# Copies of a k-v product moved ahead of a turned q, and six stores split in two

One NeuronCore of a Trainium2 chip runs the kernel. The metric is the device time of one execution in microseconds. The span in a profile is the time from the first to the last recorded instruction, some 1.8 us less. Times with three decimals are read from the trace's records, where the views round to two.

In the text and the profile lines, PE is the matmul engine, ScalarE (ACT) and VectorE (DVE) are the engines that copy and compute, GpSimd (POOL) is a fourth, and SP is the engine that issues most of the transfers (DMA). PSUM is the memory in which the PE leaves its results. A semaphore is a counter on which an instruction can wait; a wait is "held" while its counter is not there yet and "met" once it is. A transfer "lands" when its semaphore has its last update.

## The reference

Linear attention with cosine weights, then a SwiGLU block, over 4608 tokens:

```python
# q, k, v: (8, 8, 576, 64) float32; w_gate, w_val: (512, 1536); w_out: (1536, 512)
r = np.maximum(x, 0.0); phi = concat([r * cos_w, r * sin_w], axis=-1)    # for q and for k
kv = einsum('bhsf,bhsd->bhfd', k_p, v);  z = sum(k_p, axis=2)
attn = einsum('bhsf,bhfd->bhsd', q_p, kv) / (einsum('bhsf,bhf->bhs', q_p, z)[..., None] + 1e-06)
g = x @ w_gate                     # x: attn as (4608, 512)
out = (g / (1 + exp(-g)) * (x @ w_val)) @ w_out
```

## The kernel before

The program is laid out by hand: each engine executes its instructions in the order in which the code emits them. Two places matter.

The first is the end of the first group of tokens, where the second batch (b=1) gets ready. `kv_mm` makes its k-v products on the PE, `qturn_pe` turns its q on the PE and copies the turned q out of PSUM, `kv_out` copies the products out, and `a_half` multiplies the two:

```python
def qturn_pe(b, j, lo, hi, eng):
    ps = take(1) ...
    for c in range(lo, hi):
        nc.tensor.transpose(out=ps[:, c - lo], in_=st["qp"][:, b, c, j], identity=ident)   # L274
    copy_op(eng, qt_of(b)[...], ps[...])                                                   # L333
...
def kv_out(b, engs=("act", "dve"), js=slice(0, J)):
    for e, eng in enumerate(engs):
        for i in range(2):
            (nc.scalar.copy if eng == "act" else nc.vector.tensor_copy)(out=kvd[...], in_=ps[...])  # L297
...
at("b11", lambda: kv_mm(1), q_(1, 0, 0), q_(1, 1, 0, "dve"), lambda: kv_out(1))
at((0, 0), lambda: kv_free(1), a_(4, 0), a_(4, 1))
```

The second is the output. There are 36 tiles of 128 tokens. Each is copied from PSUM into one of four buffers `ob` and stored in two halves by SP. The last tile is made in two column pieces, each stored by SP and ScalarE together:

```python
obp = ctx.enter_context(tc.tile_pool(name="obp", bufs=4))
...
def ffn_out(t, f0=0, f1=None):
    ...
    (nc.scalar.copy if t % 2 == 0 else nc.vector.tensor_copy)(out=ob, in_=ps)                # L556
    for e in range(2):
        idx = 2 * t + e
        nc.sync.dma_start(out=out_v[idx // NC, idx % NC], in_=ob[e * SH:(e + 1) * SH])       # L559

def ffn_out_last(t):
    for lo, hi in ((0, 320), (320, d_model)):
        ...
        nc.scalar.copy(out=ob[:, 0:hi - lo], in_=ps)                                         # L571
        for e in range(2):
            idx = 2 * t + e
            (nc.sync if e else nc.scalar).dma_start(...)                                     # L574
```

The framework gives each transfer from SP and ScalarE one of eight semaphores, in turn. At the very end SP waits for all of them, first to eighth, one wait instruction each.

## Time and profile before

| | before |
|---|---|
| median of the runs beside the changed kernel | 324.99 us (324.85 to 325.15, 4 runs) |
| span of the profiled run | 323.204 us |
| PE busy | 98% |
| L549 goes on after the eight L444 of the first tile of batch two | 42.954 us |
| end of the last matmul | 319.219 us |
| last store lands | 321.850 us |
| from there to the end of the span | 1.354 us |

The PE is busy for 98% of the span, and it bounds the kernel but for a few places. So a gain must show in one of three numbers: the time at which L549 goes on after 41 us, the time between the last matmul and the last landing, or the time from that landing to the end. The prediction shows the lines of the profile from which these are read.

### The profile page before, as it was taken

The numbers are of one execution on the slowest core, as the hardware profiler recorded it, in microseconds if no ns is written. First come the engines' busy times: TensorE is split into PE (matmuls) and PEld (weight loads), VectorE is DVE, ScalarE is ACT, GpSimd is POOL, SyncE is SP. The second block draws the span as 40 slices with busy tenths as digits, with TensorE's granted clock in tenths as the row PEclk, the third lists the DMA queues.
The fourth block names the chain that finished last, engine by engine and source line by source line (L and its number), as shares of the span: only waits on it lengthen the run. The fifth ranks groups of instructions, "written<-read, shape, count | busy, mean of one in ns | idle before, by whom it ended". The sixth has DMA issues, their size and how long they took to land.

```text
span 323.2 us, 6031 instructions
## 1 busy us (share of the span) xinstructions
PE 316.1 (98%) x2384; PEld 159.0 (49%) x2384; DVE 180.9 (56%) x363; ACT 130.7 (40%) x239; POOL 35.3 (11%) x60
## 2 busy tenths in 40 slices
PE   7899999999999999999999999999999999999995
PEld 3596555454445444544454445444544444444443
DVE  7873766787448747564756555755573236323320
ACT  7553546662436345333533354335432132213311
POOL 6755002010101000110011000200000000000000
PEclk9999999999999999999999999999999999999999
DMA  7999997987995988599679968895912401240014
GB/s 267 215 200 197 206 194 136 213 113 108 178 200 79 184 152 134 79 175 177 116 97 160 164 123 118 134 184 109 134 36 48 103 14 35 50 103 11 0 32 97
DMA packets 74379, 41.01 MB, mean 127 GB/s; under 512 B 49904, under 2 KB 69104, under 8 KB 74352
## 3 DMA queue, kind: packets, MB, share of 16 engines
q1 hardware_dynamic: 52000, 22.95, 38.9%
q0 software_dynamic: 22192, 17.57, 36.6%
q8 instruction: 18, 0.29, 0.4%
q10 hardware_dynamic: 160, 0.13, 0.1%
q14 instruction: 9, 0.07, 0.1%
HBM read 37.75 MB, written 9.44 MB: 146 GB/s over the span
## 4 chain that ended last, share of the span: by engine, by line
PE 95%; ACT 2%; DVE 2%; issue 0%; ACTq 0%
PE banks L513 58%; PE banks L549 28%; PE banks L285 3%; PE banks L399 2%; PE banks L444 1%; PE banks L381 1%; DVE v L239 1%; PE banks L152 1%; PE banks L568 1%; PE banks L325 0%; PE banks L485 0%; ACT L184 0%; ACT phit L333 0%; PE banks L274 0%; ACT ob L571 0%; DVE qwT L369 0%
## 5 line engine op out<-in xcount | busy, mean ns | idle before, releaser
L524 DVE TENSOR_TENSOR ht<-sg,banks 128x512 bf16<-128x512 bf16 (+2 forms) x116 | 74.7, 650 | 68.7 <-PE banks L513 60.3
L513 PE MATMUL banks<-xT,wv_sb 128*128 128x512 bf16 (+2 forms) x464 | 111.3, 364 | 0.0
L513 PE MATMUL banks<-xT,wg_sb 128*128 128x512 bf16 (+2 forms) x464 | 111.3, 364 | 0.0
L519 ACT ACTIVATE sg<-banks 128x512 bf16<-128x512 f32 (+2 forms) x116 | 65.8, 568 | 111.6 <-PE banks L513 107.7
L549 PE MATMUL banks<-wo_sb,ht 128*128 128x512 bf16 x420 | 93.8, 379 | 0.0
L513 PEld LDWEIGHTS <-wv_sb 128*128 128x128 bf16 x464 | 44.8, 98 | 48.7
L513 PEld LDWEIGHTS <-wg_sb 128*128 128x128 bf16 x464 | 43.1, 98 | 42.8
L549 PEld LDWEIGHTS <-ht 128*128 128x128 bf16 x420 | 40.3, 98 | 45.7 <-issue 0.2
L556 ACT COPY ob<-banks 128x512 f32<-128x512 f32 x18 | 10.6, 586 | 54.0 <-PE banks L549 54.0
L235 DVE TENSOR_TENSOR r_q<-raw_q,tab 128x1152 bf16<-128x1152 bf16 x24 | 17.9, 754 | 20.7 <-ACT raw_q L218 20.7
L556 DVE COPY ob<-banks 128x512 f32<-128x512 f32 x17 | 11.7, 691 | 28.6 <-PE banks L549 28.6
L239 DVE TENSOR_TENSOR v<-raw_v,tab 128x1152 bf16<-128x1152 bf16 x31 | 22.8, 753 | 0.1
L421 DVE TENSOR_TENSOR x<-banks,rec 128x512 bf16<-128x512 f32 (+1 forms) x32 | 21.6, 674 | 1.3 <-PE banks L381 0.3
L218 ACT ACTIVATE raw_k<-raw_k 128x576 bf16<-128x576 bf16 (+1 forms) x25 | 17.1, 694 | 0.0
L218 ACT ACTIVATE raw_q<-raw_q 128x576 bf16<-128x576 bf16 x24 | 15.5, 679 | 0.0
L729 POOL COPY hold<-phit 1x2 bf16<-1x2 bf16 x5 | 0.9, 175 | 129.6 <-DMA phit<-r_q 129.6
L399 PEld LDWEIGHTS <-phit 128*128 128x128 bf16 (+1 forms) x240 | 10.0, 100 | 6.5 <-issue 1.3
L399 PE MATMUL banks<-kv,phit 128*128 128x65 bf16 (+1 forms) x240 | 11.6, 195 | 0.0
L152 PE MATMUL banks<-zeros 128*128 128x64 bf16 (+1 forms) x64 | 8.5, 292 | 1.0 <-DVE zeros L147 1.0
L308 DVE CAST kv<-banks 64x260 bf16<-64x260 f32 x12 | 5.1, 428 | 7.4 <-ACT kv L308 7.3
L285 PEld LDWEIGHTS <-raw_k 64*64 64x64 bf16 x504 | 7.6, 106 | 3.0 <-issue 2.1
L285 PE MATMUL banks<-v,raw_k 64*64 64x130 bf16 x504 | 8.8, 218 | 0.0
(84 smaller groups left out, 130.9 us busy)
## 6 DMA issues: line engine op xcount, KB each, us to landing
out_dram<-ob SPq DMA_DIRECT2D x70, 128.0 KB, 2.4
raw_k<-in_k_dram POOLq DMA_DIRECT2D x7, 576.0 KB, 9.1
raw_q<-in_q_dram POOLq DMA_DIRECT2D x6, 576.0 KB, 6.3
raw_v<-in_v_dram POOLq DMA_DIRECT2D x6, 576.0 KB, 12.0
wo_sb<-in_moe_w_out_dram POOLq DMA_DIRECT2D x3, 512.0 KB, 13.0
wg_sb<-in_moe_w_gate_dram POOLq DMA_DIRECT2D x5, 256.0 KB, 8.6
wv_sb<-in_moe_w_val_dram POOLq DMA_DIRECT2D x5, 256.0 KB, 9.2
wo_sb<-in_v_dram SPq DMA_DIRECT2D x2, 576.0 KB, 4.3
```

The costliest lines, as they stand in the source:

```text
L152: nc.tensor.matmul(out=ps, lhsT=zeros, rhs=zeros[:, 0:cols].unsqueeze(1).to_broadcast([P, 4, cols]), start=True, stop=True)
L218: nc.scalar.activation(out=out, in_=in_, func=AF.Relu)
L235: nc.vector.tensor_tensor(out=st[b, "q"][:, g], in0=o.unsqueeze(2).to_broadcast([P, NC, 2, D]), in1=tab, op=ALU.mult)
L239: nc.vector.tensor_tensor(out=v2s[b % 2][:, g, :, :, 0:D], in0=(first if b == 0 and g == 0 else {"v": raw_of(b, "v")})["v"][:, g].unsqueez ...
L285: nc.tensor.matmul(out=ps[i * D:(i + 1) * D, e, j * 2 * D1:(j + 1) * 2 * D1], lhsT=raws[b, "k"][es, g, c], rhs=v2s[b % 2][es, g, c, :, 0:D ...
L399: nc.tensor.matmul(out=ps[ms, e, g * D1:(g + 1) * D1], lhsT=phit[b][:, e, g, c:c + n].rearrange("p c s -> p (c s)"), rhs=kv2s[b % 2][:, e, ...
L421: nc.vector.tensor_tensor(out=st["x", t].rearrange("p (y e d) -> p e y d", e=2, d=D)[:, :, ys], in0=ps[:, :, 0:2 * J * D1].rearrange("p e ...
L513: nc.tensor.matmul(out=st["f", tg, fc, lo][i], lhsT=(wg_sb, wv_sb)[i][:, kc, fs], rhs=xT[tg][:, ts, kc], start=(kc == 0), stop=(kc == KC - 1))
L519: nc.scalar.activation(out=sg[:, 0:n], in_=st["f", tg, fc, lo][0], func=AF.Silu)
L524: nc.vector.tensor_tensor(out=hts[tg % 2][:, fc, r:r + n], in0=st.pop(("s", tg, fc, lo))[:, 0:n], in1=ps[1], op=ALU.mult)
L549: nc.tensor.matmul(out=o_ps[t], lhsT=hts[tg % 2][:, fc, r:r + P], rhs=wo_sb[:, fc], start=(fc == 0), stop=(fc == FC - 1))
L556: (nc.scalar.copy if t % 2 == 0 else nc.vector.tensor_copy)(out=ob, in_=ps)
```

## The change

The intent is to let the products leave PSUM while the PE is still turning q, and to shift the last four stores along the eight semaphores, so that SP has most of its closing waits behind it when the last store lands.

```diff
@@ ffn_out
-            nc.sync.dma_start(out=out_v[idx // NC, idx % NC], in_=ob[e * SH:(e + 1) * SH])
+            parts = 2 if NH - 10 <= idx < NH - 4 else 1
+            for i in range(parts):
+                cols = slice(i * d_model // parts, (i + 1) * d_model // parts)
+                nc.sync.dma_start(out=out_v[idx // NC, idx % NC][:, cols], in_=ob[e * SH:(e + 1) * SH, cols])
@@ ffn_out_last
-                (nc.sync if e else nc.scalar).dma_start(...)
+                (nc.scalar if e else nc.sync).dma_start(...)
@@ the plan
-    at("b11", lambda: kv_mm(1), q_(1, 0, 0), q_(1, 1, 0, "dve"), lambda: kv_out(1))
+    at("b11", lambda: kv_mm(1), lambda: kv_out(1), q_(1, 0, 0), q_(1, 1, 0, "dve"))
```

More of the change, by code (lines that the diff above doesn't have):

```diff
@@ L573, in ffn_out_last @@
                 idx = 2 * t + e
-                (nc.sync if e else nc.scalar).dma_start(out=out_v[idx // NC, idx % NC][:, lo:hi],
+                (nc.scalar if e else nc.sync).dma_start(out=out_v[idx // NC, idx % NC][:, lo:hi],
                                                         in_=ob[e * SH:(e + 1) * SH, 0:hi - lo])
```

## The prediction

> **What bounds the kernel now.** I read four views of the profile of before, from the whole to the two places that the change touches. First the page: the span, and the chain that ended last.
>
> ```profile
> span 323.2 us, 6031 instructions
> ...
> PE 95%; ACT 2%; DVE 2%; issue 0%; ACTq 0%
> ```
>
> The kernel is a string of matmuls. A change is worth only what it takes from the few places where the PE stands still, or from what stands before the first and after the last matmul. The granted clock is 0.998, so no throttling is to be won back. Second, the chain in order of time, between 38 and 56 us (start, length, what):
>
> ```profile
> 38.88 1.27 PE banks L285 x69
> 40.15 0.51 PE banks L274 x7
> 40.66 0.02 issue
> 40.69 0.91 ACT phit L333
> 41.59 0.27 ACT kvd L297
> 41.87 0.01 issue
> 41.88 0.38 ACT kvd L297
> 42.26 0.04 issue
> 42.30 0.72 PE banks L444 x7
> 43.02 1.83 PE banks L549 x8
> ```
>
> This is the place of the first part. L285 makes the k-v products of batch two (b=1 in the code), L274 turns its q on the PE, L333 copies the turned q out of PSUM, L297 copies the products out, and L444 is the first attention tile that needs all of them. From 40.66 to 42.30 the chain is not on the PE but on ScalarE, which takes the copy of q first, though the products were finished half a microsecond earlier. After 43.02 the chain is on the PE to the end of the matmuls. Third, the timeline of that stretch (start, length, engine, line):
>
> ```profile
> 40.69 0.91 ACT L333 COPY phit<-banks 128x896 bf16<-128x896 bf16 x1 [1.34 <-PE banks L274]
> 40.88 1.03 PE L549 MATMUL banks<-wo_sb,ht 128*128 128x512 bf16 x4
> 41.08 0.63 DVE L333 COPY phit<-banks 128x896 bf16<-128x896 bf16 x1 [0.77 <-PE banks L274]
> 41.49 0.76 ACT L297 CAST kvd<-banks 64x260 bf16<-64x260 f32 x2
> 41.62 0.86 DVE L297 CAST kvd<-banks 64x260 bf16<-64x260 f32 x2
> 41.83 0.30 PE L444 MATMUL banks<-kvd,phit 128*64 128x260 bf16 x1
> 42.30 0.72 PE L444 MATMUL banks<-kvd,phit 128*64 128x260 bf16 x7 [0.17 <-ACT kvd L297]
> ```
>
> The PE is not idle all that time: four matmuls of L549 fill 40.88 to about 41.83. What it loses is the gap from the first L444 (41.83) to the other seven (42.30), and another within these. ScalarE stood idle for 1.34 us and VectorE for 0.77 us before their copies of q. Fourth, the end: the timeline, and SP's closing waits from 321.86 on.
>
> ```profile
> 319.40 0.32 ACT L571 COPY ob<-banks 128x192 f32<-128x192 f32 x1 [0.71 <-PE banks L568]
> 319.75 0.50 ACTq L574 DMA_DIRECT2D out_dram<-ob  x1
> ```
>
> ```profile
> L815 SPq EVENT_SEMAPHORE  x8: 27/28/28, 321.9 to 322.3; - x8
> ```
>
> In the trace's records the last store (ScalarE's) lands at 321.850 and SP's first held wait passes at 321.867. Seven more waits follow one by one, the eighth at 322.301: (322.301 - 321.867) / 7 = 0.062 us each. All seven had long been met. They name the hardware-DMA semaphores in order, first to eighth, and the store that lands last is on the first. So SP is held at the head of the list and then reads the rest of it for nothing.
>
> **What the Trainium skill says.** "PSUM — Partial Sum Buffer", section "Engine vs sequencer instructions", says that the queues of ScalarE and VectorE are strict FIFO. The trace agrees: L297 stood behind L333 until 41.49, with its input there from 40.15. "Perfetto Trace Analysis", section "Identifying Dependency Chains", says that an instruction that waits on several engines may have EventSemaphore instructions put in front of it. The trace agrees: the eight above, and on ScalarE one at 319.319 ahead of the last copy. "DMA: Bandwidth & Descriptors", section "Anatomy of one DMA", lays most of the fixed cost of a transfer, about 2.0 us on the GpSimd path, to the receipt of the write. The trace's stores from SP and ScalarE agree in kind: 48 KB take 1.9 and 2.1 us to landing, 128 KB 2.4 us. Size hardly counts, so halving six stores gains nothing by itself.
>
> **The first part, step by step.** Nothing is added or removed; on each of ScalarE and VectorE one copy of q changes places with two copies of products.
> - ScalarE has 0.91 + 0.76 us to do, about 1.57 us with the overlap that the trace shows (40.69 to 42.25). Before, it starts when the seven transposes are done (40.66). After, it can start when the products are done (40.15, seen by ScalarE at about 40.19): products to 40.95, then q, whose transposes are long done, to about 41.8. So it ends about 0.47 us earlier.
> - VectorE: its L524 multiply runs to 40.31, so products from 40.33 to 41.2, then q (its transposes end at 41.06) to about 41.8; before it ended at 42.48. Gain 0.65 us, more than needed.
> - The PE's first L444 then waits for the copy of q, near 41.8 to 41.9, against 41.83 before, and the other seven follow without a gap. Before, the last of the eight starts at 42.749 and L549 goes on at 42.95. Later tiles show that such matmuls follow about 0.11 us apart, and those of half the columns in pairs, so eight take about 0.4 us: last start near 42.25, L549 near 42.47. **Gain 0.47 us**, between 0.35 and 0.6.
> - Is it kept? The chain is on the PE from 43.02 to 318.24. What the PE waits for then comes from ScalarE and VectorE, which the same matmuls drive and which move along. Transfers: the PE's waits for turned x are met over 3 us before the first matmul that uses it (at 151.45 the PE's sequencer waits 0.4 us for one, but the products start at 155.36), and the w_out parts have 1.9 us at 44.91. I count the whole gain as kept.
>
> **The second part.** Tiles 31, 32 and 33 are stored as four pieces instead of two: six stores more.
> - Issue: SP takes 0.47 to 0.60 us a store. Tile 33's copy ends at 314.75; four stores end near 317.0, and tile 34's copy ends at 317.23. They fit, barely; the others have far more room. None delays the last ones.
> - Semaphores: the DMA issues of the page add up to 122 hardware transfers (6 loads, 42 transposes, 74 stores), and the records show that these take eight semaphores in turn. 122 = 15 x 8 + 2, so the last four fall on the seventh, eighth, first and second. With 128 they fall on the fifth to eighth. The swap of SP and ScalarE gives ScalarE, whose last store landed 0.24 us after SP's (321.850 against 321.612), the eighth. Then six waits pass early, the seventh is met at about 321.6 and the eighth is the last: seven waits after the landing go away, 7 x 0.062 = **0.43 us**.
> - Against it: the last copy on ScalarE reuses the buffer of tile 32, now with four stores to wait for instead of two. One more wait instruction stands between ScalarE's issue of the first piece (to 319.28) and the copy at 319.40: about 0.06 us, on the path. Net **0.37 us**.
>
> Sum: 0.47 + 0.37 = 0.84 us. 325.12 - 0.84 = 324.28; I say 324.3 us.
>
> **Rivals.**
> 1. A wait takes the place of the removed one: the tile then waits for q as it waited for products. For it: ScalarE has the same 1.57 us to do either way. Against it: it starts 0.47 us earlier, and that is all I count. If its copies run slower beside VectorE's and the transposes, 0.2 us are left; time 324.55.
> 2. The gain is made and lost before 54.7 us, where VectorE is busy 8.79 of 11.6 us and one pair of L444 at 49.19 takes 0.28 instead of 0.22 us, having waited for VectorE. Against it: VectorE's chain there starts from the same attention tile and moves with it. Then only the stores count: 324.75.
> 3. The order of closing waits is not kept, or the swapped stores land later: ScalarE's store with other rows, or a landing order in which the seventh comes last. Then the second part gives between -0.1 and +0.3 us: 324.35 to 324.75.
> 4. Both parts fail: 325.1. A part that does harm: four stores of tile 33 run late and hold up tile 34 and the last ones by about 0.5 us at SP; time 324.8.
>
> **Range and chances.** The three runs of before lie within 0.3 us, which is a third of the gain, so the low end is 324.3 less noise and a kinder first part, 323.85, and the high end is where one part fails, 324.85. Faster by 2% would be 6.5 us, eight times all that either part can reach; slower by 2% would need a new stall of that size, which no view hints at. Same: 0.99.
>
> **What would show each step.** Right: ScalarE's L297 starts near 40.2 and its L333 of 128x896 near 40.9; the eight L444 stand in one piece from about 41.85, and L549 goes on near 42.45; the first matmul of the last group comes some 0.5 us before 308.83. At the end: SP's last held wait is followed by the drain within 0.1 us, instead of 0.5; 78 stores from SP and 80 in all, against 72 and 74. Wrong: L297 starts early but L549 still goes on after 42.8; the gain of 0.5 us at 43 us is no longer there at 308 us; the held wait is not the eighth; or ScalarE's last copy starts more than 0.2 us after its matmuls end.

## The result

The changed kernel took 324.48 us (median of 4 runs, 324.36 to 324.65) against 324.99 us (4 runs): 0.51 us less. The ratio is 0.9985, with a 95% interval of 0.9967 to 1.0002. Such a ratio is the mean time of one kernel's fast runs over that of the other's of the same rounds, so it is not quite the ratio of the medians. The interval reaches past 1, so these runs alone do not show a gain; the traces do.

The chain in order of time of the changed kernel (start, length, what), which answers to the chain of before in the prediction:

```profile
40.18 0.04 issue
40.22 0.38 ACT kvd L297
40.60 0.01 issue
40.61 0.37 ACT kvd L297
40.98 0.02 issue
41.01 0.91 ACT phit L333
41.92 0.04 issue
41.97 0.63 PE banks L444 x8
42.60 1.83 PE banks L549 x8
```

The copies have changed places, the eight L444 stand in one piece, and the chain is back on L549 at 42.60 instead of 43.02. (By the start of its first matmul: 42.531 instead of 42.954.) Those 0.42 us are kept: the last matmul ends at 318.799 instead of 319.219.

The end, by the timeline of the changed kernel:

```profile
318.30 0.56 ACTq L577 DMA_DIRECT2D out_dram<-ob  x1
319.03 0.32 ACT L574 COPY ob<-banks 128x192 f32<-128x192 f32 x1 [0.76 <-DMA out_dram<-ob]
319.38 0.50 ACTq L577 DMA_DIRECT2D out_dram<-ob  x1
```

(The changed kernel has three more lines, so what was L571, L574 and L815 before is L574, L577 and L818 here. The bracket of the last copy names a store; but the stores of tile 32, whose buffer the copy reuses, had all landed by 315.492, so that store did not hold it.) The last copy starts at 319.028, 0.229 us after the last matmul's end. Before, it was 0.178 us. The last store lands at 321.496 us, 0.354 us earlier than before. But the span is 322.854 us: from the landing to the end are 1.358 us, against 1.354 before. The six waits that have moved ahead of the landing have not shortened the end at all. SP's closing waits from 321.5 us on show where the time is (from left: line, queue, operation, count, shortest, median and longest in ns, first and last start):

```profile
L818 SPq EVENT_SEMAPHORE  x2: 28/28/28, 321.5 to 321.9; - x2
L818 SPq DRAIN  x1: 33/33/33, 322.0 to 322.0; - x1
```

Two waits only, as intended, for the seventh and the eighth semaphore. The seventh passes at 321.513, 17 ns after ScalarE's store has landed on it. The eighth, SP's own store, has been met since 321.226, and should pass 0.06 us later. It starts at 321.901, after 0.388 us. Nothing that it waits for is late. The same view of before lists eight waits in 0.43 us, an even 0.06 us apart.

### The profile page after: what moved, and what is told of

The parts are those of the page before. It is cut to its first block, busy times and chain, and to the rows that moved or that the text cites. A ratio compares the mean times of both kernels' runs of the same rounds, so it can differ in the third digit from the quotient of the medians.

```text
span 322.9 us, 6033 instructions
## 1 busy us (share of the span) xinstructions
PE 316.3 (98%) x2374; PEld 159.2 (49%) x2384; DVE 181.0 (56%) x363; ACT 130.5 (40%) x239; POOL 35.1 (11%) x60
## 4 chain that ended last, share of the span: by engine, by line
PE 93%; DVE 3%; ACT 2%; DMA 1%; issue 0%; ACTq 0%
PE banks L513 58%; PE banks L549 28%; PE banks L285 3%; PE banks L399 2%; PE banks L444 1%; PE banks L381 1%; DMA out_dram<-ob 1%; DVE v L239 1%; DVE raw_k L220 1%; PE banks L485 0%; DVE qwT L369 0%; ACT L184 0%; ACT phit L333 0%; ACT kvd L297 0%; ACT tabq L181 0%
## 5 line engine op out<-in xcount | busy, mean ns | idle before, releaser
L549 PE MATMUL banks<-wo_sb,ht 128*128 128x512 bf16 x410 | 93.1, 379 | 0.5
L549 PEld LDWEIGHTS <-ht 128*128 128x128 bf16 x420 | 40.3, 98 | 45.7 <-issue 0.2
L152 PE MATMUL banks<-zeros 128*128 128x64 bf16 (+1 forms) x64 | 9.4, 309 | 1.0 <-DVE zeros L147 1.0
```

The lines of the kernel that those rows point to most:

```text
L152: nc.tensor.matmul(out=ps, lhsT=zeros, rhs=zeros[:, 0:cols].unsqueeze(1).to_broadcast([P, 4, cols]), start=True, stop=True)
L549: nc.tensor.matmul(out=o_ps[t], lhsT=hts[tg % 2][:, fc, r:r + P], rhs=wo_sb[:, fc], start=(fc == 0), stop=(fc == FC - 1))
```

## The experiments

Each ran five rounds beside the kernel before on the same chip, and all gave right results. In the next four kernels one run of before took 326.25 us, which pulls the ratios there below those of the medians. "Landing to end" is from the landing of the last store to the end of the span, in the profiled run.

**One part at a time, and the changed kernel again.**

First part alone:

```diff
-    at("b11", lambda: kv_mm(1), q_(1, 0, 0), q_(1, 1, 0, "dve"), lambda: kv_out(1))
+    at("b11", lambda: kv_mm(1), lambda: kv_out(1), q_(1, 0, 0), q_(1, 1, 0, "dve"))
```

> Only the first part: ScalarE and VectorE copy the k-v products out ahead of the turned q; the stores are as before. Theory (the gain at 43 us is kept): the last group of output products begins about 0.42 us earlier than before, the span is 322.8 us against 323.2, the time 0.4 us under before. Rival (the gain is lost on the way): L549 goes on near 42.53 as in the changed kernel, but the time is within 0.1 us of before. The closing waits are as before: seven after the last landing, some 0.43 us.

Measured: 324.47 us against 324.85, ratio 0.998 (0.9964 to 0.9996). The chain in order of time:

```profile
40.38 0.38 ACT kvd L297
40.76 0.01 issue
40.77 0.37 ACT kvd L297
41.14 0.02 issue
41.17 0.91 ACT phit L333
42.08 0.04 issue
42.12 0.63 PE banks L444 x8
42.76 1.40 PE banks L549 x6
```

In this run everything before 40 us is 0.16 us later than in the run of before, so clock times do not compare directly. From the start of ScalarE's first copy to L549 are 2.38 us, as in the changed kernel (40.22 to 42.60), and the last copy of q no longer waits for the transposes. Landing to end is 1.334 us, with its seven trailing waits. The first part by itself gives the 0.38 us.

Second part alone (the change without its last hunk):

```diff
+    at("b11", lambda: kv_mm(1), q_(1, 0, 0), q_(1, 1, 0, "dve"), lambda: kv_out(1))
-    at("b11", lambda: kv_mm(1), lambda: kv_out(1), q_(1, 0, 0), q_(1, 1, 0, "dve"))
```

> Only the second part: six more stores and the swap, the copies at 41 us as before. Theory: six of the seven closing waits that follow the last landing pass before it (6 x 0.062 = 0.37 us), and one more wait ahead of ScalarE's last copy costs 0.06 us: time 0.3 us under before, span near 322.9. Rival (a new delay at the end, of the kind that the changed kernel's trace shows as 0.39 us between the seventh and the eighth wait, belongs to the longer list of SP): the gain is 0 to 0.05 us and the 0.39 us gap is there again, at the same wait.

Measured: 325.08 us against 324.85, ratio 1.0005 (0.9984 to 1.0025): nothing, or a loss too small to tell. Landing to end 1.357 us, and 0.388 us between the last two waits, as in the rival. The gap comes with the stores of the second part, not with the copies.

Changed kernel again, unedited:

> The changed kernel once more, unedited. Its profiled run was the slowest of four (span 322.9 against 322.6 to 322.7). If the gap of 0.39 us between the last two closing waits belonged to that one run, this trace has 0.06 to 0.09 us there and a span near 322.5 to 322.6; if it belongs to the program, it is there again and the span is 322.8 to 322.9. Time 0.5 to 0.7 us under before, and the sum of what the two parts give alone.

Measured: 324.47 us against 324.85, ratio 0.998 (0.9964 to 0.9995). The gap is there again, 0.374 us, so it belongs to the program. The expected 0.5 to 0.7 us under before did not come: it is 0.38 us, the time of the first part alone.

Without the exchange of SP and ScalarE:

```diff
-                (nc.scalar if e else nc.sync).dma_start(...)
+                (nc.sync if e else nc.scalar).dma_start(...)
```

> The changed kernel without the exchange of SP and ScalarE in the last four stores: ScalarE stores the first 64 rows again. The semaphores that the four take are the same as with the exchange (ScalarE fifth and seventh, SP sixth and eighth), which the built programs show. Theory: the exchange does nothing, time within 0.1 us of the changed kernel. Rival (which rows an engine stores sets when they land): a difference of 0.2 us or more, and ScalarE's last store lands at another distance from its issue than 2.12 us.

Measured: 324.51 us against 324.85, ratio 0.9982 (0.9966 to 0.9998). ScalarE's last store lands 2.12 us after its issue starts, SP's 1.86 us, as in the changed kernel (2.12 and 1.85). The exchange does nothing: the rows do not set when a store lands, and the semaphores are the same either way. Whether the later landing belongs to ScalarE as the issuer or to being second is not shown: in the last two pairs of stores of every trace here, ScalarE's issue starts 4 to 5 ns after SP's.

**What the gap belongs to.** The traces offered a lead. In all five traces read so far (before, changed, first part, second part, changed again), a packet of 8 KB on the queue that fetches instructions (number 14) starts 1.00 to 1.03 us after the 207th instruction that SP records. In the changed kernel that instruction is the wait for the seventh semaphore, and the gap follows it. In before, the 207th is SP's last. The packets of the window from 321.4 us to the end, in the DMA view of the changed kernel (queue, kind, packets, MB, share):

```profile
q14 instruction: 1, 0.01, 2.2%
```

The same view of the kernel before from 321.8 us to its end has no packet; its own comes at 324.173, after the end of the span. So the theory was that SP goes from one block of its instruction stream to the next there, and that this costs it some 0.3 us. The rival was that the gap belongs to the eighth wait, or to a wait that comes after a held one. Two kernels tell these apart. In the first the six extra stores are issued by ScalarE, so SP's list is as long as before:

```diff
-                nc.sync.dma_start(out=out_v[idx // NC, idx % NC][:, cols], in_=ob[e * SH:(e + 1) * SH, cols])
+                (nc.scalar if i else nc.sync).dma_start(
+                    out=out_v[idx // NC, idx % NC][:, cols], in_=ob[e * SH:(e + 1) * SH, cols])
```

> The changed kernel, but the six extra stores are issued by ScalarE, so SP's list is as long as before (207 recorded instructions instead of 213) while the last four stores keep the fifth to eighth semaphore. In all five traces so far an 8 KB instruction packet follows SP's 207th recorded instruction by 1.00 to 1.03 us, and in the kernels with six more stores SP stands 0.37 to 0.39 us between the 207th and the 208th, which are the last two closing waits. Theory (SP crosses a block of its instruction stream there, after its 207th instruction): no gap between the seventh and eighth wait, 0.06 us instead of 0.38, span near 322.4, time 0.3 us under the changed kernel, 324.15. Rival (the gap belongs to the eighth wait, or to a wait that follows a held one): the gap of 0.38 us is still there and the time is that of the changed kernel, 324.45.

Measured: 324.15 us against 324.89, ratio 0.9975 (0.9963 to 0.9988). SP's closing waits from 321.50 us:

```profile
L818 SPq EVENT_SEMAPHORE  x2: 28/28/28, 321.5 to 321.6; - x2
L818 SPq DRAIN  x1: 7/7/7, 321.7 to 321.7; - x1
```

The same two waits on the same semaphores, the first held by the same store, and now 0.062 us apart. Landing to end is 0.962 us. The theory holds. A part of this kernel's gain has nothing to do with the gap. ScalarE's end, by its timeline from 317.5 us:

```profile
318.39 0.50 ACTq L577 DMA_DIRECT2D out_dram<-ob  x1
319.06 0.32 ACT L574 COPY ob<-banks 128x192 f32<-128x192 f32 x1 [0.70 <-DMA out_dram<-ob]
```

The issue of the first piece takes 0.50 us where it took 0.56 in the changed kernel. So the last copy starts 0.173 us after the last matmul's end instead of 0.229, with the same two wait instructions ahead of it. Why the issue is shorter is not shown.

In the second, eight stores are split. The last four are then back on the semaphores of before, and SP's list is eight recorded instructions longer than before:

```diff
-            parts = 2 if NH - 10 <= idx < NH - 4 else 1
+            parts = 2 if NH - 12 <= idx < NH - 4 else 1
```

> The changed kernel with eight extra stores on SP instead of six: the last four stores are back on the semaphores of before (seventh, eighth, first, second), so seven waits stand behind the landing, and SP's list is eight longer. Theory (a fixed place in SP's stream): the gap of 0.37 us stands between SP's 207th and 208th instruction, which here are the waits for the fifth and the sixth semaphore, and between the last two there is 0.06 us. Time 0.4 us over the kernel with only the copies exchanged: 324.85. Rival (the gap belongs to the eighth wait): it is between the last two again.

Measured: 325.07 us against 324.89, ratio 1.0008 (0.9995 to 1.002). SP's closing waits, from 321.50 to 321.90 us and from 322.20 to 322.40 us:

```profile
L818 SPq EVENT_SEMAPHORE  x5: 28/28/28, 321.6 to 321.8; - x5
...
L818 SPq EVENT_SEMAPHORE  x3: 28/28/28, 322.2 to 322.4; - x3
```

Five waits, then 0.374 us, then three. The gap stands between the 207th and the 208th recorded instruction, here the waits for the fifth and the sixth semaphore. Between the last two there are 0.059 us. So it has moved two waits up the list, as a fixed place in SP's stream demands and the rival forbids. With both the gap and the seven trailing waits, landing to end is 1.724 us. The time is 0.22 us above the expected 324.85, in runs that scatter from 324.85 to 325.76.

**The intended gain by other means.** Products first, no split stores, no exchange; the two stores of tile 29 go out by GpSimd, whose transfers use other semaphores. Two hardware transfers fewer shift the last four as six more do:

```diff
-            nc.sync.dma_start(out=out_v[idx // NC, idx % NC], in_=ob[e * SH:(e + 1) * SH])
+            (nc.gpsimd if t == 29 else nc.sync).dma_start(out=out_v[idx // NC, idx % NC], in_=ob[e * SH:(e + 1) * SH])
```

> Products first, no extra stores, no exchange; instead the two stores of tile 29 go out by GpSimd, so two fewer hardware transfers: the last four fall on the fifth to eighth semaphore, with a list on SP that is three shorter and only two stores to wait for ahead of ScalarE's last copy. Theory: all of the gain that the second part was meant to have, six waits of 0.062 us, and no gap: time 0.37 us under the kernel with only the copies exchanged, 324.1, span 322.3. Rival (waits behind the last landing were never worth anything, something else holds the end): 324.4 to 324.5.

Measured: 324.31 us against 324.89, ratio 0.9982 (0.9969 to 0.9996), with a spread of 324.09 to 324.69. In the trace landing to end is 0.990 us and the last two waits are 0.061 us apart, as expected. The time falls between the theory's 324.1 and the rival's 324.4, so it does not decide by itself.

The same with the last copy on VectorE:

```diff
-            nc.scalar.copy(out=ob[:, 0:hi - lo], in_=ps)
+            copy_op("dve" if lo else "act", ob[:, 0:hi - lo], ps)
```

> As the one before, and the very last copy out of PSUM is done by VectorE, which is idle, while ScalarE is still issuing its store of the first piece. In the changed kernel ScalarE's copy starts 0.21 us after its matmuls end. Theory: the copy starts within 0.05 us of the matmuls' end and takes 0.32 us or a little more, so the end comes another 0.1 to 0.2 us earlier: time 323.95. Rival (VectorE's copy takes 0.1 to 0.2 us longer, which eats the gain): 324.1.

Measured: 324.23 us against 324.89, ratio 0.9977 (0.9965 to 0.999). The copy starts 0.092 us after the last matmul's end instead of 0.181, and takes 0.358 us instead of 0.320. The 0.05 us that remain are less than the runs scatter; the expected 0.1 to 0.2 us was too much.

**The best of these side by side,** on one chip: the changed kernel a third time, the kernel with the extra stores on ScalarE again, and that with the last copy on VectorE (the two edits above together).

> The changed kernel a third time, as the measure for the next two on the same chip. The theory (a block boundary of SP's instructions between the last two closing waits): the gap of 0.37 to 0.39 us is there again, time 0.4 to 0.5 us under before.

> The kernel with the six extra stores on ScalarE, unedited, beside the changed kernel on one chip. Theory: 0.3 us under the changed kernel, 0.7 under before. If the two are within 0.1 us, what the earlier call showed was the chip's doing.

> As the one before, with the very last copy out of PSUM on VectorE, whose waits for the buffer of tile 32 lie in its idle time instead of behind ScalarE's issue. Theory: the last copy starts 0.1 us after the matmuls' end instead of 0.2 us and takes 0.36 us instead of 0.32, so 0.1 us is won: 0.1 us under the one before. Rival: nothing, within 0.05 us.

| kernel | time | before, same rounds | ratio (95%) | landing to end |
|---|---|---|---|---|
| changed | 324.35 | 324.88 | 0.9983 (0.9971 to 0.9996) | 1.334 |
| extra stores on ScalarE | 324.10 | 324.88 | 0.9975 (0.9963 to 0.9988) | 0.967 |
| and last copy on VectorE | 323.94 | 324.88 | 0.9972 (0.9958 to 0.9985) | 0.981 |

The gap of the changed kernel is there a third time (0.374 us). Moving its six stores to ScalarE gives 0.25 us by the medians, and the end of the span follows the landing 0.37 us sooner. Another 0.06 us of the profiled run's gain is the earlier copy, 0.172 us after the last matmul instead of 0.230, as in the first run of this kernel. The last step is 0.16 us by the medians, but from the last matmul to the end of the span the profiled runs differ by 0.04 us only (3.628 and 3.590); the copy starts 0.093 us after the last matmul instead of 0.172. The intervals of the three ratios all overlap. The last kernel beats both: 323.94 us, 0.94 us under before and 0.41 us under the changed one, and all five of its runs (323.88 to 324.25) are below all five of the changed kernel (324.29 to 324.45).

## Why the prediction was right, and where it was not

324.48 us lies in the range (323.85 to 324.85), but the sum of 0.84 us was not what happened: one of its two terms was right and the other came to nothing. That the time lies in the range is in part the range's doing: its high end was set where one part fails, which is what happened. And the sum was taken from 325.12 us, one run of before; from the median of 324.99 it would have been 324.15.

**The first part was right.** It foresaw ScalarE's first copy of products at 40.19, and it came at 40.22; L549 near 42.47, and it came at 42.53. The gain is 0.42 us instead of 0.47. The small difference is an overlap: the prediction let the copy of q begin 0.1 us before the copy of products ended, as the copy of products does behind that of q in the trace of before. After the change it begins 0.03 us behind it (end of the products' copy at 40.98, start at 41.01). So the copy of q ended at 41.92 instead of about 41.8; the eight L444 then took a little less than was reckoned. Rival 2, that the gain is lost before 54.7 us, fell: it is 0.42 us at 42.5 us and 0.42 us at the last matmul, and the first part alone accounts for 0.38 us of time.

**The cost of one more wait was right.** Ahead of ScalarE's last copy stand two wait instructions instead of one. The copy starts 0.229 us after the last matmul's end instead of 0.178: 0.05 us, where the prediction had 0.06. This copy meets one of the prediction's signs of being wrong ("more than 0.2 us after its matmuls end"). But the 0.178 us of before and the 0.06 that it reckoned with are already 0.24, so that sign could not tell right from wrong.

**The step on the semaphores failed, twice.** First in a detail: "The swap of SP and ScalarE gives ScalarE ... the eighth." It does not. The built programs give ScalarE the fifth and the seventh and SP the sixth and the eighth with the exchange or without it, and the traces agree; why the framework deals them out so is not shown. So the last held wait is the seventh, which was one of the prediction's signs of being wrong; one wait is left behind the last landing instead of none, and six are saved, 0.37 us instead of 0.43. Then in substance: "seven waits after the landing go away, 7 x 0.062 = 0.43 us" took each closing wait at the 0.062 us of the row from which it was read. That holds for the instructions of that list at their old places. Six more stores also move them six places along SP's stream, and the wait for the eighth semaphore came to stand just behind a place at which SP stops for 0.31 to 0.33 us (0.374 to 0.388 in the traces, less 0.062). In the profiled run of the changed kernel it was 0.326 us, and the two drains (SP's next instructions) came 0.05 us later in all. That is 0.376 us against the 0.372 saved by six waits: landing to end 1.358 us against 1.354.

Put together for the two profiled runs: 0.42 us from the copies, less 0.05 us for the extra wait, less 0.015 us from the start of the last copy to the landing, less 0.004 us from there to the end, is the 0.35 us by which the spans differ. All that the second part did shows in the stretch from the end of the last matmul to the end of the span: 3.985 us before and 3.976 with the first part alone, but 4.055, 4.043 and 4.049 in the three traces of the changed kernel and 4.060 with the second part alone. With the extra stores on ScalarE it is 3.605 and 3.628. The medians differ by 0.38 to 0.53 us; with runs that scatter by 0.3 us that is no contradiction.

Rival 3 ("the order of closing waits is not kept, or the swapped stores land later") comes nearest for the second part. It even names "a landing order in which the seventh comes last", which came true, but that cost one wait of 0.06 us; the rest is the stop. That SP may be stopped by the length of its own list was not among the rivals. It could have been: the trace of before has a stop of this kind already, 128 recorded instructions earlier. SP's timeline from 140 to 150 us:

```profile
139.19 9.28 SPq L497 DMA_TRANSPOSE xT<-x  x3
149.00 1.10 SPq L559 DMA_DIRECT2D out_dram<-ob  x2
```

Between these two rows lies a wait instruction that the view leaves out. SP's 79th ends at 148.467 and its 80th, a wait met 24 us before, starts at 148.916: 0.449 us, where after the transpose before that the pause is 0.045 us. In all thirteen traces it is 0.446 to 0.459 us. The chain lies on the PE at that time, so it cost nothing there, and the prediction never looked at pauses that no wait explains.

**What is shown and what is not.** That the stop is tied to a fixed place in SP's list is shown by the six traces with a 208th instruction on SP (lists of 213 and 215), where it follows the 207th whatever that one is, and by the edit that shortens the list to 207 and leaves the last four semaphores as they are: there the stop is gone. (With the two stores on GpSimd the list has 204, and there is no stop either.) That it is the passage to a new block of instructions is inferred from the 8 KB packet, which follows the 207th instruction by 1.00 to 1.13 us in each of the eleven traces that have one. The packet comes after the stop, not in it, so these would be instructions for later. The inference has two weak points. The queue carries ten such packets in an execution, far more than SP's two stops, so they are not SP's alone. And at the first stop the next one comes 1.6 to 2.5 us after the end of the 79th. What exactly SP does in the 0.31 to 0.33 us stays open.

## What to carry to other kernels

Work that is ready should not stand behind work that is not, in an in-order queue: look for an engine idle ahead of one copy while the input of the next has already landed. When instructions are added to an engine whose end is on the path, count where its list then ends, and look in the trace of before for pauses between two instructions that no wait explains (here after the 79th and the 207th; no run shows whether other lists have such places). If a shift of a list is wanted for its semaphores, put the extra instructions on an engine that is idle, not on the one that closes the program: here that was worth 0.25 us by the medians.

## What the Trainium skill lacked or had wrong

- "Runtime: NRT & Kernel Launch", section "Instruction fetch mechanics", says of an instruction block's boundary: "The cost of crossing a 16 KiB boundary is one DMA tail-bump, mostly hidden." If SP's stop is such a crossing, which is inferred and not shown, it was not hidden at the end of the program: 0.37 to 0.39 us instead of 0.06 us ahead of a wait that was already met, in all of the six traces in which the 208th instruction is in the span.
- That section also gives blocks of 16 KiB, 256 instructions. The packets of the queue (number 14) that the stops point to are of 8 KB, and the two stops in SP's list lie 128 recorded instructions apart (the 79th and the 207th). At the 64 bytes that "Perfetto Trace Analysis", section "The 4-stage abstract model", gives for an instruction, 8 KB are 128. Packets of 16 KB are there too, on another queue (number 8).
- No page that I read says how far apart two like stores land that SP and ScalarE issue together. Two of 48 KB, SP's issued 4 ns ahead, landed 1.85 us after the start of issue from SP and 2.12 us from ScalarE, and the same with the rows exchanged. SP's was always the first, so issuer and order are not told apart.
